# Identity columns of the transposed keys written on the chip, second buffers cleared by ScalarE, first fills and key return due later

## The chip, the core and the metric

The kernel runs on one core of one Trainium2 chip. A core has five engines with instruction queues of their own: TensorE (PE; its weight loads are listed apart as PEld), VectorE (DVE), ScalarE (ACT), GpSimd (POOL) and SyncE (SP), whose queue issues most of the transfers. The transfers run on 16 DMA engines. An engine takes its instructions in the order in which the program names them. The metric is the device time of one execution in microseconds.

## What is computed

Three stages in float32, cut to what matters:

```python
for t in range(S):                      # stage 1: B, H, S, D = 4, 8, 768, 40
    m_new = maximum(f[t] + m, i[t])
    f_stab, i_stab = exp(f[t] + m - m_new), exp(i[t] - m_new); m = m_new
    C = f_stab * C + i_stab * outer(v[t], k[t])      # D x D for each of the 32 heads
    n = f_stab * n + i_stab * k[t]
    y[t] = sigmoid(o[t]) * (C @ q[t]) / maximum(abs(n . q[t]), 1)
x = y as 3072 tokens x 320
logits = x @ w_gate                     # stage 2: 8 experts, 384 tokens each
# all (token, expert) pairs in the order of falling logits: a token takes the first
# expert that still has room
x = relu(x[of expert e] @ w1[e]) @ w2[e]             # 320 -> 1024 -> 320
h = x @ w_in                            # stage 3: 320 -> 2048 -> 320
out = (maximum(h, 0) + alpha * minimum(h, 0)) @ w_out
```

## The kernel before

Stage 1 is `attention()`. The sequence is cut into 9 chunks of L = 86 steps (NCH = 9). A unit is one chunk of one batch entry; 36 units run in order, four to a chunk, and `score(u)`, `value(u - 2)`, `turn(u - 4)` and the rest of the loop's body are issued for each. Within a chunk the recurrence is a masked product, and the state C that enters a chunk is carried as 40 extra rows beside the 86 steps. So the transposed keys KT of a chunk have X = 126 columns for each of 16 pairs of heads: 86 keys, then a 40 x 40 identity that picks the state. A matmul of KT and Q gives pS, VectorE multiplies it by the weights W (ScalarE's exponential of pE, itself a product of cE and aE), and a matmul with V gives pY.

Buffers: Q and KT have R = 2, V has 3, aE and cE have 3. Pairs of heads share one matmul, so Q has zeros where the other head's rows stand, and partitions 80 and up of KT are zero. A load writes 80 partitions of KT; memsets before the first loads clear the rest: for buffer 0 by GpSimd and VectorE (lines 334 to 338), for buffer 1 by GpSimd (lines 385 and 386). In the kernel before, the host lays out `h_kt` with the 40 identity columns in it, and `load_qk(c)` (line 359) loads 80 rows of 16 x 126 numbers, 8064 contiguous bytes each.

The gates are prepared by `gates()`, a generator with a `yield` after each step, in three pieces: chunk 0 (`g0`), chunks 1 to 3 (`g1`) and the rest (`g2`). A piece is a chain on VectorE (two scans, differences, a maximum) and then three times a copy to bf16 on ScalarE (line 298) and a subtraction of it (line 302). The loop over `g0` (from line 387) inserts `fill_a(0)` and `fill_c(0)`, VectorE's copies of the constant rows into aE[0] and cE[0] (lines 373 and 377). Then come `load_a(0)`, three small transfers of `ap` into three rows of aE[0] issued by SP (line 316), `gates_rows(0)` (matmuls, then ScalarE's copy into cE[0], line 312), `prep(0)` (VectorE's copy of the identity `vid` into KR[0], line 347), two more `fill_c`, SP's loads for the next chunk, `fill_a(1)` and the first G0 = 7 steps of `g1`, all before unit 0. SP issues in this order too: q, k and v of chunk 0, the aE rows, kr, og, v, q and k of chunk 1. Later chunks' loads are issued from the units' loop; from unit 8 on, the loop also loads and converts halves of stage 3's weights (`r`, `convert()`).

Stages 2 and 3 are `rest()`. The assignment runs in rounds (`rounds()`), one for each expert: `bisect()` searches the threshold over the table `key`, `pick()`, `compact()` and `gather()` fetch the expert's tokens (xg), `kill()` and `choose()` prepare the next round. `choose()` writes the new keys to DRAM and reads them back in another layout (lines 699 and 700). Beside it TensorE runs the expert's MLP and then the final MLP for its tokens, f from 0 to NF - 1 = 15, with `turn_x()` transposing the next expert's tokens at the last three f. The order of both is written by a planner: `tp` and `td` are its reckoning of TensorE's and VectorE's time, `mm()` adds a matmul to `tp`, and `due()` says whether the next step of the round is issued now. After `choose()` a round yields `keys_at - tp`, so that the next step is issued when `tp` has reached `keys_at`. `rest()` sets `need`, the due time, to `tp` before the first expert, whatever was yielded. If the next expert's gather has not been issued at f = NF - 4, the round is stepped out there, and after it five more microseconds of planned VectorE work.

Of the kernel before, what the change touches and what calls it, by code (L numbers as in the profile page):

```python
# [9 lines left out]
F32 = mybir.dt.float32  # L10
# [78 lines left out]
def host_layout(inp):  # L89
# [8 lines left out]
    def dmajor(a):  # L98
        a = chunks(a).reshape(B, 4, 2, NCH, L, D).transpose(3, 2, 5, 0, 1, 4)
        return np.ascontiguousarray(a).reshape(NCH, 2, D, 16, L)  # L100
# [2 lines left out]
        return np.ascontiguousarray(chunks(a).transpose(2, 3, 0, 1, 4))  # L103

    o["h_q"] = dmajor(q)
    kt = np.zeros((NCH, 2, D, 16, X), np.float32)
    kt[..., :L] = dmajor(k)
    kt[..., L:] = np.eye(D, dtype=np.float32)[:, None, :]
    o["h_kt"] = kt.reshape(NCH, 2 * D, 16, X)
    o["h_kr"] = rows(k).reshape(NCH, L, 32, D)  # L110
    ve = np.ones((NCH, L, 32, D + 1), np.float32)
    ve[..., :D] = rows(v).reshape(NCH, L, 32, D)
# [50 lines left out]
class Kern:  # L163
# [154 lines left out]
    def attention(self):  # L318
        nc, a, tc = self.nc, self.a, self.tc
        with ExitStack() as ctx:  # L320
# [14 lines left out]
            nc.vector.memset(Q[0][:, 1], 0.0)  # L335
            self.gates_fill()
            nc.gpsimd.memset(KT[0][64:], 0.0)
            nc.gpsimd.memset(V[0][64:], 0.0)
            ident = self.identf
            vid = p.tile([128, D], F32, name="vid")  # L340
            nc.vector.tensor_scalar(vid, jp, 0.0, None, op0=OP.is_equal)
            pm = p.tile([128, H * (D + 1)], I32, name="pm")
            wg = p.tile([128, 3, 32], F32, name="wg")
            OG = {}
# [10 lines left out]
            def load_qk(c):  # L355
                r = c % R
                for s in range(2):
                    nc.sync.dma_start(Q[r][D * s:D * s + D, s], a["h_q"][c, s])
                nc.sync.dma_start(KT[r][:2 * D], a["h_kt"][c])

            def load_v(c):
                rows(V[c % RV], a["h_v"][c])
# [9 lines left out]
            def fill_a(r):  # L372
                nc.vector.tensor_copy(self.aE[r].rearrange("p b h l -> p b (h l)"),
                                      self.ae0[:, None, :].to_broadcast([KE, B, H * L]))
# [7 lines left out]
            g0 = self.gates(0, 1, nc.vector)  # L382
            g1 = self.gates(1, 4, nc.vector)
            g2 = self.gates(4, NCH, nc.gpsimd)
            nc.gpsimd.memset(Q[1], 0.0)
            nc.gpsimd.memset(KT[1][64:], 0.0)
            for i, _ in enumerate(g0):
                if i == 4:
                    fill_a(0)
                    fill_c(0)  # L390
            self.load_a(0, nc.sync)
            self.gates_rows(0, ps)
            prep(0)
            fill_c(1)
            fill_c(2)
# [281 lines left out]
    def choose(self, keys, at=320):  # L677

        nc, p, v = self.nc, self.bp, self.v
        B3 = [128, E, 24]  # L680
        self.mine = p.tile([128, 24], F32, name="mine")
        ch = self.rb[:, at:at + 192].rearrange("p (e j) -> p e j", e=E)
        v.tensor_reduce(self.best, self.Lm.rearrange("p e j -> p j e"), axis=AX.X, op=OP.max)
        yield DVE
        v.tensor_tensor(ch, self.Lm, self.best[:, None, :].to_broadcast(B3), op=OP.is_equal)
        yield DVE
        v.tensor_tensor(ch, ch, self.ew[:, :, None].to_broadcast(B3), op=OP.mult)
        yield DVE
        v.tensor_reduce(self.mine, ch.rearrange("p e j -> p j e"), axis=AX.X, op=OP.max)
        if not keys:  # L690
            return
        yield DVE
        v.tensor_tensor(ch, ch, self.mine[:, None, :].to_broadcast(B3), op=OP.is_equal)
        yield DVE
        v.tensor_scalar(ch, ch, 0.5, 2 * OUT, op0=OP.subtract, op1=OP.mult)
        yield DVE
        kt = p.tile(B3, F32, name="ky")
        v.tensor_tensor(kt, ch, self.Lm, op=OP.min)
        nc.sync.dma_start(self.kd.rearrange("e (p j) -> p e j", j=24), kt)
        nc.sync.dma_start(self.key, self.kd.rearrange("e (g t) -> (e g) t", t=192))  # L700
        self.keys += 1
        self.keys_at = self.tp + 5.6

    def count(self, src, thr, op, col=0):
        self.td -= 0.07
# [620 lines left out]
```

## Time and profile before

| | us |
|---|---|
| three runs | 817.33, 814.41, 822.41 |
| median | 817.33 |
| the profiled execution | 814.77 |
| its span, first to last instruction | 812.8 |
| mean granted TensorE clock | 0.959 of full speed |

The profile is of one execution. Attention ends near 177 us, the first round of the assignment fills the time to about 230 us, and the MLPs with the other rounds beside them the rest. A page of the profile sums each engine's busy time; a timeline lists instructions; the chain of waits is followed back from the last instruction of a stretch to what released each; a table by stretch adds the granted clock and what the DMA engines did. DMA shares are of all 16 engines. A packet is one piece that one DMA engine moves.

### The profile page before, as it was taken

To read this page: it belongs to the slowest core of one execution; us is meant where nothing else is said; L and a number is where in the kernel's file an instruction comes from. 1 tells how busy PE (TensorE), PEld (TensorE's weight loads), DVE (VectorE), ACT (ScalarE), POOL (GpSimd) and SP (SyncE) were. 2 spreads that over 40 slices of the span, in tenths; PEclk is the share of its full clock that TensorE was granted. 3 is DMA by queue.
4 is the path that set the end of the run, shared out by engine and by line. 5 is a ranking of instruction groups with operands and counts; after the bars stand their busy time and mean duration, and the time that the engine had idled before them with its cause. 6 is when DMAs were issued, how large, how long until landed. Compare 5 with 4: busy or idle time off the path is not lost.

```text
span 812.8 us, 14924 instructions
## 1 busy us (share of the span) xinstructions
PE 726.5 (89%) x4868; PEld 688.1 (85%) x4868; DVE 566.5 (70%) x2209; ACT 430.2 (53%) x945; POOL 425.9 (52%) x509
## 2 busy tenths in 40 slices
PE   3999998850199999999999999999999999999996
PEld 2998988840088988998999899999989999999996
DVE  8886786889788879877876887787788832322321
ACT  3575565658343564466267436625842764654453
POOL 5565554659572466157239516732950785634133
PEclk9999998975599999999999999999999999999999
DMA  7888988643050041032005003201400333100000
GB/s 177 201 233 218 229 217 222 188 122 108 1 193 2 1 154 65 0 113 83 25 29 167 25 2 112 83 26 42 154 25 1 127 127 100 42 1 25 1 1 25
DMA packets 36730, 74.57 MB, mean 92 GB/s; under 512 B 14576, under 2 KB 18672, under 8 KB 36652
## 3 DMA queue, kind: packets, MB, share of 16 engines
q1 hardware_dynamic: 33532, 64.74, 28.6%
q0 software_dynamic: 2688, 8.65, 3.3%
q8 instruction: 38, 0.62, 0.3%
q14 instruction: 40, 0.33, 0.1%
q10 hardware_dynamic: 432, 0.22, 0.1%
HBM read 64.04 MB, written 9.34 MB: 90 GB/s over the span
## 4 chain that ended last, share of the span: by engine, by line
PE 53%; DVE 15%; POOL 11%; issue 9%; DMA 7%; ACT 3%; SPq 0%; POOLq 0%; DVEq 0%; ACTq 0%
PE ph L1024 22%; PE acc L1024 10%; PE fo L1024 9%; PE pY L461 5%; POOL gl L1161 4%; DVE scr L158 4%; DVE rb L158 3%; PE pS L445 3%; POOL wt L1000 3%; DMA r<-in_h_wf_dram 2%; DMA aE<-ap 2%; POOL w_dt_float32r L957 1%; DVE g L158 1%; DMA k<-in_h_kt_dram 1%; POOL w_dt_float L928 1%
## 5 line engine op out<-in xcount | busy, mean ns | idle before, releaser
L1161 POOL TENSOR_TENSOR gl<-g,gh 128x384 fp32r<-128x384 f32 x127 | 128.0, 1014 | 225.1 <-ACT gh L1160 217.1
L1000 POOL TENSOR_TENSOR wt<-raw,wt 128x384 fp32r<-128x384 f32 (+1 forms) x128 | 118.2, 941 | 32.4 <-ACT wt L999 32.2
L1024 PE MATMUL ph<-yh,wfh 128*128 128x384 f32 x384 | 133.1, 347 | 0.0
L1024 PE MATMUL ph<-yh,w_dt_float32r 128*128 128x384 f32 x360 | 122.1, 339 | 0.0
L1024 PE MATMUL fo<-wfh,gh 128*128 128x320 f32 x384 | 116.4, 313 | 0.4 <-ACT gh L1160 0.4
L158 DVE SCALAR_TENSOR_TENSOR g<-ph,m 128x384 f32<-128x384 f32 x128 | 70.3, 555 | 65.3 <-ACT m L1154 57.7
L1160 ACT ACTIVATE gh<-g 128x384 fp32r<-128x384 f32 x127 | 66.0, 523 | 88.5 <-DVE g L158 88.4
L1024 PE MATMUL fo<-w_dt_float32r,gh 128*128 128x320 f32 x360 | 109.3, 312 | 0.0
L1024 PE MATMUL ph<-xh,wt 128*128 128x384 f32 x384 | 99.5, 343 | 0.6 <-ACT xh L1055 0.6
L1086 ACT ACTIVATE hh<-ph 128x384 fp32r<-128x384 f32 x64 | 31.5, 493 | 115.2 <-PE ph L1024 94.0
L1024 PE MATMUL acc<-hh,wt 128*128 128x384 f32 x320 | 89.1, 343 | 0.0
L1024 PE MATMUL ph<-yl,wfh 128*128 128x384 f32 x256 | 84.1, 339 | 0.0
L1024 PE MATMUL fo<-wfh,gl 128*128 128x320 f32 x384 | 80.1, 312 | 0.5 <-POOL gl L1161 0.5
L1154 ACT ACTIVATE m<-m,al 128x384 f32<-128x384 f32 x119 | 73.4, 617 | 3.9
L1153 ACT ACTIVATE m<-ph 128x384 f32<-128x384 f32 x119 | 57.4, 483 | 32.7 <-PE ph L1024 31.5
L1024 PEld LDWEIGHTS fo<-wfh,gh 128*128 128x128 f32 x384 | 72.2, 188 | 3.0 <-ACT m L1154 1.5
L1024 PEld LDWEIGHTS ph<-yh,wfh 128*128 128x128 f32 x384 | 72.4, 188 | 0.6 <-issue 0.2
L1024 PEld LDWEIGHTS ph<-xh,wt 128*128 128x128 f32 x384 | 69.0, 188 | 1.8 <-issue 1.0
L999 ACT ACTIVATE wt<-raw 128x384 fp32r<-128x384 f32 x128 | 62.8, 514 | 12.6 <-DMA raw<-in_h_we_dram 12.5
L1024 PEld LDWEIGHTS fo<-w_dt_float32r,gh 128*128 128x128 f32 x360 | 67.9, 188 | 1.1 <-issue 1.0
L1024 PEld LDWEIGHTS ph<-yh,w_dt_float32r 128*128 128x128 f32 x360 | 67.9, 188 | 0.7 <-issue 0.7
L461 PEld LDWEIGHTS pY<-v,dk 126*126 126x126 f32 (+1 forms) x576 | 67.2, 191 | 0.7
(237 smaller groups left out, 1636.1 us busy)
## 6 DMA issues: line engine op xcount, KB each, us to landing
raw<-in_h_we_dram SPq DMA_DIRECT2D x64, 384.0 KB
r<-in_h_wf_dram SPq DMA_DIRECT2D x32, 352.0 KB
k<-in_h_kt_dram SPq DMA_DIRECT2D x9, 630.0 KB
xd<-x SPq DMA_DIRECT2D x36, 120.0 KB
q<-in_h_q_dram SPq DMA_DIRECT2D x18, 215.0 KB
v<-in_h_v_dram SPq DMA_DIRECT2D x9, 410.0 KB
og<-in_h_o_dram SPq DMA_DIRECT2D x9, 400.0 KB
kr<-in_h_kr_dram SPq DMA_DIRECT2D x8, 400.0 KB
```

The source lines that it names most:

```text
L158: return f(out, *args, **kw)
L445: nc.tensor.matmul(pS[:, 2 * j:2 * j + 2, :], KT[r][:, 4 * b + 2 * s + j, :], Q[r][:, :, 4 * b + 2 * s + j, :], start=True, stop=True)
L461: nc.tensor.matmul(pY[:M, h, :], dk[:, h, :M], V[c % RV][:, 8 * b + h, :], start=True, stop=True)
L928: nc.gpsimd.tensor_tensor(w, w, sg, op=OP.mult)
L999: nc.scalar.activation(w[:, :384], r, AF.Copy)
L1000: nc.gpsimd.tensor_tensor(w[:, 384:], r[:, :n], w[:, :n].bitcast(F32), op=OP.subtract)
L1024: self.nc.tensor.matmul(out, w, x, **kw)
L1086: nc.scalar.activation(hh, ph, AF.Relu)
L1153: nc.scalar.activation(m, ph, AF.Relu, scale=-1.0)
L1154: nc.scalar.activation(m, m, AF.Copy, scale=alpha)
L1160: nc.scalar.activation(gh, g, AF.Copy)
L1161: nc.gpsimd.tensor_tensor(gl, g, gh.bitcast(F32), op=OP.subtract)
```

## The change

The host no longer puts the identity into `h_kt`; its rows hold 16 x 86 numbers, and the load writes 16 pieces of 86 numbers to each of 80 partitions, beside the columns 86 to 125 that it leaves alone. The chip writes the identity: VectorE adds two blocks of the 128 x 128 identity into `idk`, GpSimd copies it into KT[0] after that buffer's memset, ScalarE into KT[1]. The clears of Q[1] and of KT[1]'s partitions 64 to 127 go from GpSimd to ScalarE (a copy scaled by zero), the first ahead of the gates of chunk 0, the second behind `gates_rows(0)`. `vid` is computed by GpSimd instead of VectorE. In the loop over `g0` the two fills move back: `fill_a(0)` from step 4 to 5 and `fill_c(0)` from step 4 to 7. In `choose()` the due time of the next round becomes the later of `tp` and `td` plus 6.6 instead of `tp` plus 5.6.

```diff
--- before.py
+++ after.py
@@ -103,10 +103,7 @@
         return np.ascontiguousarray(chunks(a).transpose(2, 3, 0, 1, 4))
 
     o["h_q"] = dmajor(q)
-    kt = np.zeros((NCH, 2, D, 16, X), np.float32)
-    kt[..., :L] = dmajor(k)
-    kt[..., L:] = np.eye(D, dtype=np.float32)[:, None, :]
-    o["h_kt"] = kt.reshape(NCH, 2 * D, 16, X)
+    o["h_kt"] = dmajor(k).reshape(NCH, 2 * D, 16, L)
     o["h_kr"] = rows(k).reshape(NCH, L, 32, D)
     ve = np.ones((NCH, L, 32, D + 1), np.float32)
     ve[..., :D] = rows(v).reshape(NCH, L, 32, D)
@@ -335,10 +332,13 @@
             nc.vector.memset(Q[0][:, 1], 0.0)
             self.gates_fill()
             nc.gpsimd.memset(KT[0][64:], 0.0)
+            ident = self.identf
+            idk = p.tile([2 * D, D], F32, name="idk")
+            nc.vector.tensor_tensor(idk, ident[:2 * D, :D], ident[:2 * D, D:2 * D], op=OP.add)
+            nc.gpsimd.tensor_copy(KT[0][:2 * D, :, L:], idk[:, None, :].to_broadcast([2 * D, 16, D]))
             nc.gpsimd.memset(V[0][64:], 0.0)
-            ident = self.identf
             vid = p.tile([128, D], F32, name="vid")
-            nc.vector.tensor_scalar(vid, jp, 0.0, None, op0=OP.is_equal)
+            nc.gpsimd.tensor_scalar(vid, jp, 0.0, None, op0=OP.is_equal)
             pm = p.tile([128, H * (D + 1)], I32, name="pm")
             wg = p.tile([128, 3, 32], F32, name="wg")
             OG = {}
@@ -356,7 +356,7 @@
                 r = c % R
                 for s in range(2):
                     nc.sync.dma_start(Q[r][D * s:D * s + D, s], a["h_q"][c, s])
-                nc.sync.dma_start(KT[r][:2 * D], a["h_kt"][c])
+                nc.sync.dma_start(KT[r][:2 * D, :, :L], a["h_kt"][c])
 
             def load_v(c):
                 rows(V[c % RV], a["h_v"][c])
@@ -382,14 +382,17 @@
             g0 = self.gates(0, 1, nc.vector)
             g1 = self.gates(1, 4, nc.vector)
             g2 = self.gates(4, NCH, nc.gpsimd)
-            nc.gpsimd.memset(Q[1], 0.0)
-            nc.gpsimd.memset(KT[1][64:], 0.0)
+            zero = ident[:, 1:2]
+            nc.scalar.activation(Q[1].rearrange("p s g l -> p (s g l)"), zero.to_broadcast([128, 32 * L]), AF.Copy, scale=0.0)
             for i, _ in enumerate(g0):
-                if i == 4:
+                if i == 5:
                     fill_a(0)
+                if i == 7:
                     fill_c(0)
             self.load_a(0, nc.sync)
             self.gates_rows(0, ps)
+            nc.scalar.activation(KT[1][64:].rearrange("p g x -> p (g x)"), zero[64:].to_broadcast([64, 16 * X]), AF.Copy, scale=0.0)
+            nc.scalar.activation(KT[1][:2 * D, :, L:], idk[:, None, :].to_broadcast([2 * D, 16, D]), AF.Copy)
             prep(0)
             fill_c(1)
             fill_c(2)
@@ -699,7 +702,7 @@
         nc.sync.dma_start(self.kd.rearrange("e (p j) -> p e j", j=24), kt)
         nc.sync.dma_start(self.key, self.kd.rearrange("e (g t) -> (e g) t", t=192))
         self.keys += 1
-        self.keys_at = self.tp + 5.6
+        self.keys_at = max(self.tp, self.td) + 6.6
 
     def count(self, src, thr, op, col=0):
         self.td -= 0.07
```

## Rows read from the trace of the kernel before

**Rows 1.** page: busy time, share, instructions; DMA busy in tenths of 40 slices

```profile
PE 726.5 (89%) x4868; PEld 688.1 (85%) x4868; DVE 566.5 (70%) x2209; ACT 430.2 (53%) x945; POOL 425.9 (52%) x509
...
DMA  7888988643050041032005003201400333100000
```

**Rows 2.** TensorE's waits, 44 to 140 us: total us, times, longest us

```profile
PE pE L438 <- DMA aE<-ap: 2.4, 2, 1.8
PE pS L445 <- ACT KL L517: 2.2, 1, 2.2
```

**Rows 3.** chain of waits: start us, length us, what

```profile
68.47 7.79 DMA aE<-ap
```

**Rows 4.** by stretch: busy us (instructions) each engine, clock, DMA share, GB/s

```profile
76.00:80.00 4.00, 3.61 (x16) 3.60 (x16) 1.31 (x4) 2.42 (x6) 2.67 (x4) 0.59 0.72 185
...
132.00:136.00 4.00, 4.00 (x40) 3.68 (x40) 2.25 (x8) 0.79 (x2) 2.10 (x4) 0.50 1.04 269
```

**Rows 5.** timeline, VectorE: start us, length us, line, operation, count

```profile
6.05 2.84 DVE L373 COPY aE<-ae 113x2752 bf16<-113x2752 bf16 x1
8.81 1.94 DVE L377 COPY cE<-ce 113x504 bf16<-113x504 bf16 x1
...
11.00 0.24 DVE L302 TENSOR_TENSOR cum<-cum,ap 32x86 f32<-32x86 f32 x1
...
11.97 0.81 DVE L347 COPY kr<-vid 126x1280 f32<-126x1280 f32 x1
12.71 0.47 DVE L377 COPY cE<-ce 113x504 bf16<-113x504 bf16 x2
13.11 0.86 DVE L373 COPY aE<-ae 113x2752 bf16<-113x2752 bf16 x1
...
16.22 0.68 DVE L293 TENSOR_TENSOR_SCAN cum<-keep,fg 32x258 f32<-32x258 f32 x1
```

**Rows 6.** timeline, same stretch: GpSimd, then ScalarE; idle before in brackets

```profile
4.48 1.22 POOL L338 MEMSET v<- 62x1312 f32 x1
5.76 2.40 POOL L385 MEMSET q<- 128x2752 f32 x1
...
6.15 0.27 ACT L298 ACTIVATE ap<-cum 32x86 bf16<-32x86 f32 x1 [2.22 <-DVE cum L293]
...
13.31 0.45 ACT L312 ACTIVATE cE<-pc 24x344 bf16<-24x344 f32 x1 [0.96 <-PE pc L310]
...
17.71 0.43 ACT L440 ACTIVATE W<-pE 126x344 f32<-126x344 f32 x1
```

**Rows 7.** lines by form, 0 to 180 us: busy us, mean ns, idle before

```profile
L957 POOL TENSOR_TENSOR w-1_dt_float32r<-w_dt_float,wfh 128x704 fp32r<-128x704 f32 x1 | 1.7, 1677 | 0.0
...
L956 ACT ACTIVATE wfh<-w_dt_float 128x704 fp32r<-128x704 f32 x2 | 1.6, 784 | 3.3 <-PE pk L525 3.3
...
L476 POOL COPY x<-x 86x64 f32<-86x64 f32 x35 | 10.3, 294 | 2.2
```

**Rows 8.** DMA queue of 7-10, 496-498, 230.9-231.9 us: packets, MB, share

```profile
q1 hardware_dynamic: 117, 0.65, 98.6%
...
q1 hardware_dynamic: 273, 0.74, 98.7%
...
q1 hardware_dynamic: 1040, 0.10, 71.5%
```

**Rows 9.** DMA issues, 44 to 131 us: count, KB each

```profile
k<-in_h_kt_dram SPq DMA_DIRECT2D x5, 630.0 KB
```

**Rows 10.** source line 700: who waited for it, us, times

```profile
  DVE rb L158: 3.1, 3
```

**Rows 11.** timeline: GpSimd's gather issue, then TensorE's transposes of it

```profile
358.51 0.99 POOL L973 DMA_INDIRECT xg<-xd,ids  x1
...
366.69 0.49 PE L1052 MATMUL ptr<-identf,xg 128*128 128x128 f32 x3
...
369.72 0.49 PE L1052 MATMUL ptr<-identf,xg 128*128 128x128 f32 x3
```

## What the change does to the time, told before it was run

> **What bounds the kernel now.** I read the page first. TensorE is busy for 89% of the span, and the packets keep the DMA engines seven to nine tenths busy in the first slices, where attention runs, and little after [rows 1]. So one question falls to each part: what delays TensorE in attention, and whether the long stage behind it, the two MLPs, can move at all.
>
> The waits of TensorE between 44 and 140 us come next [rows 2]. They are few; the two longest are 2.4 us for the small loads into aE and 2.2 us for ScalarE. Attention's middle is a stretch in which TensorE nearly keeps pace with the DMA queue. The chain of waits shows what is behind the first: aE, a load of three rows of `ap`, is 7.79 us under way [rows 3], because it stands in the queue behind the large loads. The table by stretch adds the price that the list of waits hides: the granted clock is 0.59 from 76 to 80 us and 0.50 from 132 to 136 [rows 4]; the first is a mixture of the two levels 2.4 and 1.2 GHz, the second is the lower one throughout. TensorE had idled shortly before both. Counted as four microseconds times what is missing to 1, the two stretches lose 1.64 and 2.00, together 3.6 us.
>
> The timeline of the start shows another limit. Until the first weights W are made at 17.71 us ScalarE waits for VectorE's gate values, and VectorE spends 2.84 us on the copy fill_a(0) and 1.94 us on fill_c(0) between cum and the rest of the gate chain; the same copies later take 0.86 us and 0.47 us for two [rows 5]. GpSimd clears the second buffers just then, Q[1] from 5.76 us on [rows 6].
>
> **The start, part by part.** Taken off GpSimd: the memsets of Q[1], 2.40 us [rows 6], and of KT[1]. Added there: the identity copy into KT[0], 80 x 640 elements, not in the trace. GpSimd's copy of 64 elements takes 294 ns and its product of 704 elements 1677 ns [rows 7]; 640 elements lie near the second, so I take 1.5 us (bounds 0.3 and 1.7). It stands before V[0]'s memset and delays that by as much, so v(0) is issued some 1.5 us later on SP, and what is queued behind it, load_a(0), waits for the gates anyway. Also moved to GpSimd is vid, read by prep alone. VectorE gets idk, one 80 x 40 addition, 0.24 us by the 32 x 86 operations of the chain [rows 5]; it lies where vid lay.
>
> VectorE's chain from the end of cum, which lets ScalarE go at 6.15 us [rows 6], to prep(0) at 11.97 us [rows 5] is 5.8 us now. Afterwards: ig 0.24, fill_a(0), two subtractions 0.48 (0.24 each), fill_c(0) 0.24 (half of 0.47), two subtractions 0.48. The identity copy pushes GpSimd's V[0] memset to end near 7.2 us, so fill_a(0) meets part of it: between 0.86 and 2.84 I take 1.5, nearer to the free one because only its first microsecond has a rival. Sum 2.94, with 0.2 for ScalarE's copies in between 3.15; prep(0) begins 2.7 us earlier. Bounds: with 2.84 for fill_a and idk waiting out half of GpSimd's 1.5 us copy besides, 0.6; with 0.86 for fill_a, 3.3.
>
> The slowing itself is what [rows 5] and [rows 6] show: 2.84 against 0.86 us for one instruction. The Trainium skill, page "SBUF — State Buffer", section "Who interferes with whom", says that a VectorE copy in a two-port mode and GpSimd block each other and that ScalarE never waits; this trace agrees with the first half (2.84 against 0.86), and no run here yet shows the second. By that rule the clears cost nothing on ScalarE but their own time, as the next sum has it too.
>
> ScalarE takes three new instructions. Its rows give 273 ns for 86 elements and 784 for 704 [rows 6, 7], hence 0.83 ns an element: 2752 elements 2.5 us, 2016 elements 1.9 us, 640 elements 0.7 us. Q[1]'s clear starts when ScalarE's table load ends, at 3.93 us (6.15 less the idle 2.22) [rows 6], and ends near 6.4, 0.25 after cum; fill_a(0) covers that. KT[1]'s two stand behind cE(0), which ends 2.7 us earlier, at 11.1: they last until 13.7. Behind them wait gates' copies for chunks 1 to 3, whose cum ends at 16.90 now [rows 5] and at 14.2 then. Cover 0.5 us; were the two twice as long, W would lose 2.1 us of the gain. load_qk(1) waits on SP for these clears; its data are used four units later. So the first W comes 2.7 us earlier, and what follows is bound by TensorE until DMA binds.
>
> **The key loads.** Nine loads of 80 rows x 8064 B become nine of 80 x 16 pieces of 344 B: 630 KB become 430, 80 packets become 1280. No such packet is in the trace, so I bound it from three stretches that hold nearly one kind each [rows 8]. Mean of a packet is 16 engines x length x share / packets. The 80-row loads (7 to 10 us): 47.3 engine-us for 0.65 MB, 13.7 B/ns. The 128-row loads (496 to 498): 31.6 for 0.74 MB, 23.4 B/ns; 129 ns for 3072 B once the small ones (273 less 0.74 MB / 3072 B) are set apart at 11 ns. 96 B packets: 11.0 ns. A line through the last two is 7.2 ns + 0.040 ns/B, 20.9 ns for 344 B. One row of a partition costs now 8064/13.7 = 589 ns. Later: if only bytes count, 5504/13.7 = 402; if the crowding of 80-row loads (1.74, the ratio of 23.8 to 13.7) stretches all of a packet, 16 x 36.4 = 582; if it stretches the bytes alone, 16 x (7.2 + 23.8) = 496. Each engine carries five rows, so a load gets shorter by 0.93, 0.03 or 0.47 us. I take 0.5.
>
> The Trainium skill, page "DMA: Bandwidth & Descriptors", section "Specifications", speaks against this edit: transfers need at least 512 B for line rate, and below it the engine reads, modifies and writes. Its sense here is a rival below. The trace does not bear it out for its smallest pieces: 96 B cost 11.0 ns [rows 8].
>
> Five of the loads are issued between 44 and 131 us [rows 9]: 5 x 0.5 = 2.5 us off the queue's lateness, out of 4.6 us of waits in [rows 2]. Of the 3.6 us of lost clock I take back 1.5: the shorter of the idle times may stop being one, the other need not. Together 4.0 us, bounds 0.2 and 8.2. What is late next is VectorE, which carries attention's end.
>
> **The keys' return.** In the rounds the next search is emitted when tp reaches keys_at. The last step leaves td about 0.4 us ahead of tp, so the new line delays it by 1.4 us (1.0 and 0.4). Three of the returns kept VectorE waiting, 3.1 us in all [rows 10]; the first is outside, because rest() overwrites the due time. In the MLPs VectorE has slack before most matmuls, so I take 0.5 us (bounds -1 and +1.5).
>
> **Sum.** The profiled execution took 814.77 us, span 812.8. 814.8 - 2.7 - 4.0 - 0.5 = 807.6 us. The median of the three runs is 817.33, 2.6 higher; on it the sum is 810.1. A median is what will stand against a median, so I say 809.5.
>
> **Rivals.** *Key loads hidden or no shorter:* the lower bound of 0.03 us. For it speaks that TensorE idles little; against it the two aE waits. 814.8 - 2.7 - 0.5 - 0.2 = 811.4 on the profile's time, 814 on the median.
>
> *The stalls vanish whole:* both waits (4.6) and all the lost clock (3.6) go. For it speaks that all stand behind the queue; against it that 2.5 us do not cover 4.6. 814.8 - 2.7 - 8.2 - 0.5 = 803.4, or 806.
>
> *Small packets dear, slower than before:* place, the queue from 44 to 131 us. If a piece of 344 B pays its bytes twice in the crowd, it costs 7.2 + 2 x 23.8 = 54.8 ns, a row 877 ns, a load 1.44 us more, five loads 7.2: 814.8 + 7.2 - 3.2 = 818.8, or 821.4. It decides from 45 ns a piece on: there 25 rows' excess (16 x 45 - 589) eats the 3.2 us. The 96 B row speaks against it, and that none of those went into the crowded rows speaks for it. It is also how the Trainium skill's 512 B rule named above would act.
>
> *Later keys reach the gather:* a gather not yet emitted three feed-forward blocks before the expert's end makes TensorE wait while the round is stepped out, then 5 us more. The third expert's first gather starts at 358.51 us, its transposes at 366.69, and one block is 3.03 us [rows 11]; the test comes near 363.6, slack 5.1 us against a delay of 1.4. It decides above 5.1 us and would give 807.6 + 5 = 812.6 or more; the delays of later rounds add up, 1.4 us each, which is why it keeps a chance.
>
> **How the numbers follow.** Forecast 0.54 (its own range 805 to 814), key loads without gain 0.22, stalls gone 0.14, dear packets 0.06, late gather 0.04. A measurement of this kernel tells about 1% from no change, 8.2 us. Faster by over that: all of stalls gone and the better part of the forecast's, 0.14 + 0.24 = 0.38. Slower by over 1% needs packets of some 65 ns (16 x 65 - 589 = 451 ns, 11.3 us over 25 rows, less 3.2) or both of the last two: 0.04. The rest, 0.58. The range 803 to 816 leaves out the dear packets and the tails.
>
> **What would show it.** Right: first W at about 15 us; fill_a(0) under 2 us; key packets of 344 B at 25 to 37 ns; the aE wait near 76 us under 1 us; no VectorE wait for a key return after the first. Wrong at the start: W still near 17 us, with ScalarE in KT[1]'s clears while gates' cum is done. Wrong in the middle: packets of 45 ns, longer waits for aE, more stretches at 0.5 clock. Wrong at the end: a wait of TensorE before the transposes of a gather.

## The result, and the profile after

| | before | after |
|---|---|---|
| median of 4 runs each, same chip (lowest to highest) | 819.87 us (814.41 to 825.80) | 808.62 us (807.25 to 809.98) |
| ratio of the times, 95% interval | | 0.9891 (0.9849 to 0.9932) |
| profiled execution: time, span, mean clock | 814.77, 812.8, 0.959 | 807.28, 805.5, 0.961 |
| first W of chunk 0 starts | 17.71 us | 14.04 us |
| first W of chunk 3 | 59.4 us | 56.9 us |
| first W of chunk 8 | 148.5 us | 138.4 us |
| first matmul of the first expert | 232.25 us | 222.60 us |
| from there to the end of the span | 580.6 us | 582.9 us |

The change makes the kernel 1.1% faster, 0.7 to 1.5% by the interval. Run again beside 29 runs of the kernel before, it gave a ratio of 0.9898 (0.9856 to 0.994). Ratios and means below leave out the few runs that were over 1.5% above the fastest of their kernel. The forecast was 809.5 us, and on the profiled execution 807.6; measured were 808.62 and 807.28. But the table says that the parts of the sum do not agree as well as the sum. In the profiled executions 3.7 us come from the start (forecast 2.7), 6.0 us more until the first expert (forecast 4.0), and 2.3 us are given back in the MLPs (forecast: 0.5 gained). -3.7 - 6.0 + 2.3 = -7.4, against 814.77 - 807.28 = 7.5.

The page of the changed kernel, the same rows as [rows 1]:

```profile
PE 722.2 (90%) x4868; PEld 684.9 (85%) x4868; DVE 562.3 (70%) x2209; ACT 434.6 (54%) x948; POOL 422.8 (52%) x509
...
DMA  8989889551320140042014004202400343100000
```

ScalarE is busy 4.4 us longer with three instructions more; the DMA engines are up to a tenth busier in most of the first slices. TensorE's busy time falls by 4.3 us with the same 4868 instructions. Most of it is the clock: between 44 and 140 us the lower level held for 10.2 us before and not at all after, and in the MLPs after for 3.4 us.

The timeline of the start (start us, length us, engine, line, operation, idle before in brackets), to be laid beside [rows 5] and [rows 6]:

```profile
3.95 2.50 ACT L386 ACTIVATE q<-identf 128x2752 f32<-128x2752 f32 x1
4.60 0.78 POOL L338 COPY k<-idk 80x640 f32<-80x640 f32 x1
5.44 1.19 POOL L339 MEMSET v<- 62x1312 f32 x1
5.47 0.33 DVE L290 TENSOR_TENSOR_SCAN cum<-keep,fg 32x86 f32<-32x86 f32 x1
5.99 1.37 DVE L373 COPY aE<-ae 113x2752 bf16<-113x2752 bf16 x1
...
7.61 0.45 DVE L377 COPY cE<-ce 113x504 bf16<-113x504 bf16 x1
...
8.30 0.81 DVE L347 COPY kr<-vid 126x1280 f32<-126x1280 f32 x1
...
10.12 1.88 ACT L394 ACTIVATE k<-identf 64x2016 f32<-64x2016 f32 x1
12.03 0.74 ACT L395 ACTIVATE k<-idk 80x640 f32<-80x640 f32 x1
13.26 0.42 ACT L295 ACTIVATE ap<-cum 32x258 bf16<-32x258 f32 x1 [0.50 <-DVE cum L290]
...
14.04 0.77 ACT L443 ACTIVATE W<-pE 126x344 f32<-126x344 f32 x2
```

fill_a(0) takes 1.37 us where it took 2.84, fill_c(0) 0.45 where it took 1.94, and prep(0) (the copy into kr) starts 3.67 us earlier. The last clear of KT[1] ends at 12.77 us, and ScalarE then waits 0.50 us for cum: the clears are covered, with half a microsecond to spare.

TensorE's waits from 44 to 140 us (total us, times, longest us), and then the two stretches of [rows 4] with a third one (stretch: length, busy us of PE, PEld, DVE, ACT, POOL with instructions, clock, DMA share, GB/s):

```profile
PE pS L448 <- DVE LT L567: 1.0, 3, 0.5
PE pS L448 <- ACT KL L520: 0.9, 1, 0.9
```

```profile
76.00:80.00 4.00, 3.86 (x33) 3.57 (x32) 2.69 (x8) 1.94 (x6) 2.16 (x4) 1.00 1.07 271
132.00:136.00 4.00, 4.00 (x37) 3.99 (x36) 1.72 (x4) 1.74 (x6) 1.51 (x2) 1.00 0.70 207
370.00:374.00 4.00, 3.55 (x13) 3.24 (x13) 2.11 (x15) 0.21 (x1) 3.22 (x5) 0.57 0.00 0
```

In this execution the wait for aE is gone from the list, that for KL fell from 2.2 to 0.9 us [rows 2], and both stretches run at the full clock, 1.00 for 0.59 and 0.50 [rows 4]. The third row is new: in the MLPs, at 370 us, the clock is 0.57. The timeline there names what came before it:

```profile
368.25 0.56 DVE L155 SCALAR_TENSOR_TENSOR g<-ph,m 128x384 f32<-128x384 f32 x1 [1.69 <-POOL gl L1164]
...
370.45 0.17 PE L721 MATMUL rb<-acc,c_blk 128*128 128x3 bf16 x1 [2.06 <-DVE rb L155]
```

TensorE waits 2.06 us for a step of the top-k search on VectorE, and that step stands behind the instruction for `g`, which had waited 1.69 us for GpSimd. That is where the later return of the keys put it. The wait for the keys themselves (line 703, line 700 before) fell from 3.1 us in three waits [rows 10] to 0.4 in one, as meant.

### The profile page after: what moved, and what is told of

The parts are those of the page before. It is cut to its first block, busy times and chain, and to the rows that moved or that the text cites. A ratio compares the mean times of both kernels' runs of the same rounds, so it can differ in the third digit from the quotient of the medians.

```text
span 805.5 us, 14932 instructions
## 1 busy us (share of the span) xinstructions
PE 722.2 (90%) x4868; PEld 684.9 (85%) x4868; DVE 562.3 (70%) x2209; ACT 434.6 (54%) x948; POOL 422.8 (52%) x509
## 4 chain that ended last, share of the span: by engine, by line
PE 49%; DVE 14%; POOL 9%; issue 8%; ACT 5%; DMA 2%; SPq 0%; POOLq 0%; DVEq 0%; ACTq 0%
PE ph L1027 23%; PE acc L1027 11%; PE fo L1027 10%; POOL gl L1164 4%; DVE scr L155 3%; DVE rb L155 2%; PE pY L464 2%; POOL wt L1003 2%; DVE g L155 2%; POOL w_dt_float32r L960 1%; ACT m L1157 1%; PE pS L448 1%; ACT gh L1163 1%; POOL w_dt_float L931 1%; ACT m L1156 1%
## 5 line engine op out<-in xcount | busy, mean ns | idle before, releaser
L1027 PE MATMUL acc<-hl,wt 128*128 128x384 f32 x192 | 66.6, 347 | 1.0 <-DVE hl L155 1.0
```

Source lines behind the costliest of these rows:

```text
L1027: self.nc.tensor.matmul(out, w, x, **kw)
```

## The experiments

The theory to be tested had three parts: the start gains by the clears' leaving GpSimd; the key loads are shorter because they carry fewer bytes, though in more packets; the later keys cost time where they were meant to gain. The rivals: the small packets gain nothing, or cost; all of the gain is the start's; the later keys gain. The runs came in three groups (the first four below; the next three and tp + 4.6; the last four), each beside 29 runs of the kernel before, median 817.07, 815.25 and 815.65 us. Ratios are to these. Every kernel computes the whole result.

### The old due time in the changed kernel

```diff
-        self.keys_at = max(self.tp, self.td) + 6.6
+        self.keys_at = self.tp + 5.6
```

> The changed kernel with the due time of the keys' return as before (tp + 5.6). By the prediction's sum the later due time saved 0.5 us, so this kernel should be 0.5 us slower than the changed one, at some 0.5 us above its 807.3 us. By the reading of the changed kernel's trace the later due time cost 2 to 2.5 us (a wait of TensorE of 2.06 us at 370 us that the kernel before does not have, and a stretch at the lower clock behind it, against 1.8 us of VectorE's waits gone), so it should be 2 us or more faster than the changed one, with no wait over 1 us in the MLPs. The waits of VectorE for the returned keys come back by both.

Measured: 807.93 us, ratio 0.9883 (0.983 to 0.9937); profiled 805.13. The MLPs take 580.8 us where they took 582.9, and TensorE's 2.06 us wait at the third return is not there. The gain of the change does not come from the third edit; whether that edit costs anything in the time lies within the interval. The expectation of no wait over 1 us in the MLPs was missed: there is one of 1.48 us at the second return of the keys. The kernel before has it too, and the changed kernel has not (in its profile the same step waits 0.21 us):

```profile
305.69 0.16 PE L718 MATMUL rb<-acc,c_blk 128*128 128x3 bf16 x1 [1.42 <-DVE rb L158]
```

### The new due time alone

```diff
-        self.keys_at = self.tp + 5.6
+        self.keys_at = max(self.tp, self.td) + 6.6
```

> The kernel before with the later due time of the keys alone. By the prediction's sum 0.5 us faster than before; by the reading of the changed kernel's trace 2 to 2.5 us slower, with attention unchanged (the last search table's transposes at 176.2 us) and a new wait of TensorE of about 2 us near the start of the third expert. A third theory: what the due time does in the MLPs hangs on where the round happens to stand, and then the difference here need not have the sign that the reverse edit has in the changed kernel.

Measured: 817.74 us, ratio 1.0014 (0.9979 to 1.005). The time does not tell it from nothing. In its profiled execution the MLPs take 581.6 us for 580.6, the wait at the second return is gone, and the timeline has the new wait at the same place of the third:

```profile
380.57 0.16 PE L718 MATMUL rb<-acc,c_blk 128*128 128x3 bf16 x1 [2.05 <-DVE rb L158]
```

So the new wait belongs to this edit and to no other, and the edit takes another wait away.

### The key loads alone

The loads of 344 B pieces in the kernel before; the identity columns of both buffers are written by GpSimd behind its memsets, the clears stay where they were.

```diff
+            idk = p.tile([2 * D, D], F32, name="idk")
+            nc.vector.tensor_tensor(idk, ident[:2 * D, :D], ident[:2 * D, D:2 * D], op=OP.add)
+            nc.gpsimd.tensor_copy(KT[0][:2 * D, :, L:], idk[:, None, :].to_broadcast([2 * D, 16, D]))
...
-                nc.sync.dma_start(KT[r][:2 * D], a["h_kt"][c])
+                nc.sync.dma_start(KT[r][:2 * D, :, :L], a["h_kt"][c])
...
+            nc.gpsimd.tensor_copy(KT[1][:2 * D, :, L:], idk[:, None, :].to_broadcast([2 * D, 16, D]))
```

> The kernel before with the key loads of 344 B pieces alone; GpSimd writes the identity columns of both buffers, its clears and the fills stay where they were. By the prediction's sum attention ends 4.0 us earlier, less what GpSimd's two added copies hold up at the start (0 to 1.5 us). If the loads alone account for what the changed kernel gained between the first W and attention's end, 6.4 us. If the gain came from the earlier start, which lets the loads be issued sooner, 0 to 1 us, and the waits for aE near 76 us and the stretches at the lower clock stay.

Measured: 811.44 us, ratio 0.9921 (0.9891 to 0.995), although the first W comes 1.1 us later (18.82), since GpSimd's two copies (0.71 and 0.81 us) delay VectorE's gate steps and fills. In the profiled execution the first expert starts at 228.12 us, 4.1 earlier, which is 5.2 behind the start, between the 4.0 of the sum and the 6.4 of the other reading. The rival that the key loads are hidden, or bring no gain, falls here. TensorE's waits, 44 to 140 us:

```profile
PE pS L446 <- ACT KL L518: 0.8, 1, 0.8
PE pE L439 <- DMA aE<-ap: 0.7, 1, 0.7
```

The wait for aE is 0.7 for 2.4 and that for KL 0.8 for 2.2 [rows 2].

### The start alone

The changed kernel with the wide loads of before and the old due time; no idk.

```diff
-            nc.gpsimd.tensor_copy(KT[0][:2 * D, :, L:], idk[:, None, :].to_broadcast([2 * D, 16, D]))
...
-                nc.sync.dma_start(KT[r][:2 * D, :, :L], a["h_kt"][c])
+                nc.sync.dma_start(KT[r][:2 * D], a["h_kt"][c])
...
-        self.keys_at = max(self.tp, self.td) + 6.6
+        self.keys_at = self.tp + 5.6
```

> The changed kernel with the key loads and the due time as before: 8064 B pieces with the host's identity, ScalarE's clears, the fills moved back, vid on GpSimd. By the prediction's sum the first W at 15.0 us and attention's end 2.7 us earlier than before; by the changed kernel's trace 3.7 us (first W at 14.0). If the earlier start also removed the waits behind the DMA queue, 6 to 10 us; if the queue takes the start's gain back because wide loads bind again, under 2 us.

Measured: 813.11 us, ratio 0.9929 (0.9899 to 0.9959). In its profiled execution the first W starts at 14.10 us, 3.6 earlier, but the first expert at 230.2, only 2.1 earlier. The waits of TensorE, 44 to 140 us, in this execution:

```profile
PE pE L440 <- DMA aE<-ap: 3.6, 3, 2.3
PE pS L447 <- ACT KL L519: 2.2, 1, 2.2
```

TensorE gets ahead of the queue and waits 3.6 us for aE, where it waited 2.4 [rows 2]. But the times do not show that the queue takes part of the start back: 0.71% of 817 is 5.8 us (3.3 to 8.3), no less than the 3.6 of the start.

### The start's two edits apart

```diff
-                if i == 4:
+                if i == 5:
                     fill_a(0)
+                if i == 7:
                     fill_c(0)
```

> The kernel before with the two first fills moved back (steps 5 and 7) alone; GpSimd clears the second buffers as before. If GpSimd's memsets beside them are what makes the fills slow, fill_a(0) still takes 2.5 us or more, fill_c(0) too is held up, and the first W comes at most 0.6 us earlier than 17.7. If the place in the order is what counts, the first W comes 2 us or more earlier.

Measured: 815.07 us, ratio 1.0001 (0.9966 to 1.0036). The first W starts at 16.71 us, 1.0 earlier: more than the 0.6 that the reading by GpSimd's memsets allowed, and half of the 2 that the other asked for.

```diff
-            nc.gpsimd.memset(Q[1], 0.0)
-            nc.gpsimd.memset(KT[1][64:], 0.0)
+            zero = ident[:, 1:2]
+            nc.scalar.activation(Q[1].rearrange("p s g l -> p (s g l)"), zero.to_broadcast([128, 32 * L]), AF.Copy, scale=0.0)
...
             self.gates_rows(0, ps)
+            nc.scalar.activation(KT[1][64:].rearrange("p g x -> p (g x)"), zero[64:].to_broadcast([64, 16 * X]), AF.Copy, scale=0.0)
```

> The kernel before with the clears of Q[1] and KT[1] on ScalarE alone; fills, vid, key loads and due time as before. If GpSimd's memsets are what makes the fills slow, fill_a(0) takes 0.9 to 1.4 us, fill_c(0) under 0.5, and the first W comes 3 us or more earlier, near 14.5. If the place of the fills is what counts, W gains under 1.5 us. The end of the attention stage follows by at most 2 us, as it did where the start alone was changed.

Measured: 812.51 us, ratio 0.9957 (0.9927 to 0.9987). The fills in the timeline, with the fills moved alone and then with the clears moved alone:

```profile
6.32 2.56 DVE L373 COPY aE<-ae 113x2752 bf16<-113x2752 bf16 x1
...
9.12 1.63 DVE L377 COPY cE<-ce 113x504 bf16<-113x504 bf16 x1
```

```profile
3.95 2.50 ACT L386 ACTIVATE q<-identf 128x2752 f32<-128x2752 f32 x1
...
6.05 0.85 DVE L373 COPY aE<-ae 113x2752 bf16<-113x2752 bf16 x1
6.82 0.27 DVE L377 COPY cE<-ce 113x504 bf16<-113x504 bf16 x1
```

Moved a step or two, the fills still meet GpSimd's memsets and take 2.56 and 1.63 us. With the clears on ScalarE they take 0.85 and 0.27 us; ScalarE's clear of 2.50 us lies beside the first 0.4 us of them. For the length of the fills it is the engine of the clears that matters, and of the two edits tested alone only this one shows in the time. The first W starts at 15.22 us, 2.5 earlier, a little short of the 3 expected, and at 14.10 with both edits (and with vid moved). In the profiled execution with the clears alone, 2.1 us above its median, the first expert starts at 232.43 us, no earlier than before; the gain of 0.4% stands in the runs' times only.

### Small packets at equal bytes

The kernel before, its host rows padded by 8 B a piece, so that the same 8064 B a row go as 16 pieces of 504 B.

```diff
-    kt = np.zeros((NCH, 2, D, 16, X), np.float32)
+    kt = np.zeros((NCH, 2, D, 16, 128), np.float32)
...
-                nc.sync.dma_start(KT[r][:2 * D], a["h_kt"][c])
+                nc.sync.dma_start(KT[r][:2 * D], a["h_kt"][c][:, :, :X])
```

> The kernel before with the same bytes of keys and identity, but loaded as 80 x 16 pieces of 504 B (the host's rows have a gap of 8 B after each piece) instead of 80 of 8064 B. By the prediction's line for pieces with crowding on the bytes alone a load gets 0.42 us longer (16 x 42 = 672 against 589 ns for a row), attention ends 2 us later over five loads. With crowding on all of a piece 0.84 us and 4 us. If the packets' own time overlaps between neighbours on one engine, so that only bytes count, no change within 1 us. If pieces under 512 B pay their bytes twice, a row is 16 x 77 = 1230 ns, a load 3.2 us longer, attention ends 10 us or more later.

Measured: 819.79 us, ratio 1.0051 (1.0024 to 1.0077), some 4 us slower. Cutting the rows costs time, and the change has to earn this back by the bytes that it leaves out. The total is what the expectation had with crowding on all of a piece (0.84 us a load, 4 us over five loads), and twice the bytes (3.2 us a load, 16 over five) is far off. But the loads have not become longer, as that sum has it: from its first to its last packet a load of 504 B pieces takes 6.3 us in the mean of nine, and a load of 8064 B rows 6.3 to 6.8 in the five profiles that have them. So the total is met by another way than the one it was reckoned from. The issue of a key load keeps SP busy for 0.60 us, where it took 0.32. SP's waits for key loads, 44 to 140 us, before and with the pieces:

```profile
SPq L906 <- DMA k<-in_h_kt_dram: 10.9, 5, 2.7
```

```profile
SPq L906 <- DMA k<-in_h_kt_dram: 14.4, 5, 3.1
```

With the narrow pieces alone this wait is 9.2 us, in the changed kernel 9.5. It does not account for the 4 us: in the four other profiles with wide loads it is 6.1 to 10.2, and all of SP's waits in the stretch add up to 44.2 us before and 43.9 with the pieces. The stretch 44 to 140 us in five kernels follows (before, this one, the key loads alone, the start alone, after; columns as above):

```profile
44.00:140.00 96.00, 89.48 (x840) 84.23 (x839) 70.10 (x194) 57.63 (x148) 53.43 (x81) 0.95 0.88 220
```

```profile
44.00:140.00 96.00, 89.53 (x826) 84.68 (x826) 68.92 (x192) 57.16 (x147) 52.47 (x81) 0.92 0.93 218
```

```profile
44.00:140.00 96.00, 92.09 (x896) 86.76 (x895) 72.79 (x201) 59.53 (x153) 56.07 (x85) 0.98 0.91 216
```

```profile
44.00:140.00 96.00, 88.49 (x813) 83.19 (x810) 69.10 (x193) 56.39 (x144) 51.40 (x79) 0.95 0.88 222
```

```profile
44.00:140.00 96.00, 92.58 (x916) 87.37 (x908) 75.57 (x211) 62.21 (x160) 56.97 (x88) 1.00 0.91 215
```

The instructions that TensorE gets through in the same 96 us rise and fall with the clock: 826 at 0.92, 840 and 813 at 0.95, 896 at 0.98, 916 at 1.00. Times 96 us, what is missing to 1 is 7.7, 4.8, 1.9, 4.8 and 0 us. These are single executions, that of the pieces (824.20 us) the second slowest of twelve, and they do not tell whether TensorE did less because of the clock or lost the clock because it had less to do.

The times of all runs, each with its own mean clock, allow an estimate. Call a run's lost clock its time multiplied by what is missing to full clock. Among the runs of the kernel before, the time grows by some 0.6 us for each us of lost clock. In the mean the pieces lose 40.3 us where the runs beside them lose 36.2, and the key loads alone 32.1 for 37.8. So some 2 of the 4 us that the pieces cost, and some 3.5 of the 6 that the key loads gain alone, go with the clock. Where the rest of the pieces' cost arises stays open.

### The due time: earlier still, and the changed kernel again

```diff
-        self.keys_at = max(self.tp, self.td) + 6.6
+        self.keys_at = self.tp + 4.6
```

> The changed kernel with the due time of the keys' return a microsecond earlier than before (tp + 4.6). If VectorE's waits for the keys are hidden, the MLPs last 580 to 581 us as with tp + 5.6 and VectorE's waits for keys grow to 4 us or more in all. If such a wait is passed on to TensorE, the MLPs get 1 to 3 us longer, with waits of TensorE for VectorE behind each return.

> The changed kernel with tp + 4.6. If the MLPs' length follows the due time, 578 to 579 us as in its first profile, and some 4 us less time than the changed kernel; if that profile was one lucky execution, 580 to 581 us like tp + 5.6 and about 2 us less.

The two others differ by the constant alone, 3.6 and 2.6, and one run is the changed kernel unaltered:

> The changed kernel with tp + 3.6. If the gain of an earlier due time goes on, the MLPs last under 578 us. If VectorE's wait for the keys (about 1 us a return more than at 4.6, 7 us or more in all) is now passed on to TensorE, 580 us or more, with waits of TensorE for VectorE's hl or g behind the returns.

> The changed kernel with tp + 2.6. By the first reading no longer than with 3.6; by the second 2 us or more longer than with 4.6, VectorE's waits for keys 10 us or more in all.

> The changed kernel once more, beside the next three, which differ from it in the due time of the keys' return alone (max(tp, td) + 6.6 here). By the reading that the later due time costs, TensorE has a wait of about 2 us in the MLPs behind the third return, as in its first profile and in the kernel with this edit alone, and the MLPs last 582 to 583 us. If that wait was the accident of one execution, it is absent.

| due time | median us | ratio (interval) | MLPs, us | VectorE's waits for keys, us (times) |
|---|---|---|---|---|
| max(tp, td) + 6.6, first | 808.62 | 0.9891 (0.9849 to 0.9932) | 582.9 | 0.4 (1) |
| the same, again | 807.96 | 0.9898 (0.9856 to 0.994) | 581.2 | 1.1 (1) |
| tp + 5.6 | 807.93 | 0.9883 (0.983 to 0.9937) | 580.8 | 2.0 (3) |
| tp + 4.6, first | 806.51 | 0.9881 (0.9844 to 0.9919) | 578.4 | 3.5 (4) |
| the same, again | 806.78 | 0.99 (0.9864 to 0.9935) | 579.2 | 3.9 (4) |
| tp + 3.6 | 811.99 | 0.996 (0.9929 to 0.9992) | 585.0 | 6.5 (6) |
| tp + 2.6 | 822.08 | 1.0062 (1.0034 to 1.009) | 597.0 | 16.5 (6) |

VectorE's waits for the keys grow the earlier the search is emitted, and the MLPs are shortest where these waits are not yet zero. Rows of the timeline show the two ends, in the changed kernel run again and at tp + 2.6:

```profile
370.40 0.16 PE L721 MATMUL rb<-acc,c_blk 128*128 128x3 bf16 x1 [2.06 <-DVE rb L155]
```

```profile
573.07 0.36 DVE L155 TENSOR_SCALAR rb<-key 128x192 int32<-128x192 int32 x1 [2.91 <-DMA key<-kd]
...
575.14 0.16 PE L721 MATMUL rb<-acc,c_blk 128*128 128x3 bf16 x1 [3.50 <-DVE rb L155]
```

Too late, and TensorE waits for a search step that stands behind the MLP's own work on VectorE; too early, and it waits for a search that waits for the keys. The first wait, 2.05 or 2.06 us at the third return, is in the three profiles with 6.6 and not in those with 5.6 or 4.6. The reverse holds for the wait at the second return: 1.33 to 1.48 us in all nine profiles with 5.6 or 4.6, and in none with 6.6. With tp + 5.6 the MLPs take 580.3 to 581.0 us in seven profiles, the kernel before among them, so that 578.4 and 579.2 lie outside this spread. The version with tp + 4.6 has the shortest spans of all, 801.7 and 801.6 us against 805.5 and 804.1; its ratio is not to be told from that of the changed kernel.

Four expectations were missed. The first run of tp + 4.6 has shorter MLPs (578.4 us) than either reading had it. The second is 1.2 us faster in the median than the changed kernel beside it, not 4. In the changed kernel run again the wait at the third return is there, but the MLPs last 581.2 us, not 582 to 583. And with tp + 3.6 TensorE's waits for `hl` and `g` do not grow: its waits for search steps do, 7.5 us in all (none over 0.9) for 4.8 with tp + 4.6.

## Why the prediction was right, and where its steps were not

**The start: mechanism right, and 0.3 or 1.0 us too small, by the execution.** In the first profile the first W comes 3.67 us earlier, beyond the bound of 3.3. From the end of cum to prep(0) the prediction set 3.15 us, and 2.50 were measured (5.80 to 8.30): fill_a(0) took 1.37 for the 1.5 assumed and fill_c(0) 0.45 for 0.24, which nearly cancel; but the subtractions of 0.24 us start 0.15 to 0.17 after one another (7.28, 7.45, 7.61), where they were counted at full length. A chain of short instructions on one engine costs their spacing, not the sum of their durations. And cum, which the prediction kept where it was, ended 0.31 us earlier (5.80 for 6.11). 0.65 + 0.31 is the missing microsecond.

But the changed kernel's start is in seven profiles (its own two, and the five with another due time). The first W comes at 14.04 to 14.07 us in three and at 14.74 to 14.76 in four, 2.95 us earlier than before and within the bound. In the four, two of VectorE's gate steps meet GpSimd's instructions, as in the changed kernel run again:

```profile
4.60 0.71 POOL L338 COPY k<-idk 80x640 f32<-80x640 f32 x1
4.68 0.73 DVE L286 TENSOR_TENSOR fg<-fg,gm 32x85 f32<-32x85 f32 x1
5.38 1.19 POOL L339 MEMSET v<- 62x1312 f32 x1
5.44 1.17 DVE L288 TENSOR_SCALAR fg<-fg 32x86 f32<-32x86 f32 x1
6.65 0.33 DVE L290 TENSOR_TENSOR_SCAN cum<-keep,fg 32x86 f32<-32x86 f32 x1
```

In the first profile the same two steps start at 4.56 us, just ahead of the copy, and at 4.83, and take 0.23 and 0.60. So the identity copy that went to GpSimd meets the gates' chain ahead of cum, which the prediction reckoned with for idk and fill_a(0) alone, and a tenth of a microsecond at the start of a step decides over 0.7 us. That vid's move brought cum forward is not shown: with vid moved and without the identity copies (the start alone) cum ends at 6.08 us, as before.

GpSimd's identity copy was taken at 1.5 us and took 0.71 to 0.82: its nearest row was a product of two inputs, and a copy is a good deal cheaper. ScalarE's clears took 2.50, 1.88 and 0.74 us for 2.5, 1.9 and 0.7 foretold, and their covers held, the second with 0.50 us left, as said.

The second half of the rule cited from the Trainium skill, page "SBUF — State Buffer", section "Who interferes with whom", that ScalarE never waits for the other two, agrees with these runs: Q[1]'s clear took 2.50 us whether GpSimd ran a memset beside it and VectorE a copy at its end (the clears alone) or GpSimd a copy and a memset (the changed kernel).

**The key loads: right direction, wrong currency.** The step took a packet's mean time for a share of the engine's time, and expected 25 to 37 ns for 344 B. Measured over the nine loads of the changed kernel were 37.8 ns, so that a row of 16 takes 605 ns, no less than the 589 of before. By that step's own rule the loads had not got shorter, and yet the kernel with narrow pieces alone is 0.8% faster, and from first to last packet a load takes 5.1 us in the mean where it took 6.4 (5.6 with the narrow pieces alone). The mean times of a packet came out near the step's line with crowding on all of it, 37.8 ns for 36.4 with 344 B and 49.7 for 47.6 with 504 B; adding them up was wrong. What the step lacked is in the queue's view (packets, MB, share of 16 engines): 7 to 8.5 us in the changed kernel, and 6.1 to 10 us in the kernel with pieces of 504 B:

```profile
q1 hardware_dynamic: 822, 0.35, 137.5%
```

```profile
q1 hardware_dynamic: 1338, 0.85, 103.2%
```

A share above 100% means that packets of one engine overlap in time. The durations of single packets can then not be added to an engine's time, and the formula of [rows 8], which gave 98.6% for the wide rows, does not carry over. A first sign of it is in [rows 4], 1.04 from 132 to 136 us, with a load of wide rows issued there. That the bytes left out do the gaining is shown by two kernels: with 16 pieces and 8064 B a row the time rises by 0.5%, with 16 pieces and 5504 B it falls by 0.8%.

On the rule cited from the Trainium skill, page "DMA: Bandwidth & Descriptors", section "Specifications" (at least 512 B for line rate): the pieces of 504 B lie below it and did cost, 0.51% (0.24 to 0.77). No run here has pieces just above 512 B, so whether it is that limit or the number of packets that costs is not told apart. A price of twice the bytes, 7.2 us more over five loads by the prediction's sum, is excluded for 344 B by the gain.

**The lost clock: counted too small before, and got back whole in one profile of seven.** The prediction counted 3.6 us from two stretches of four microseconds. By the trace the lower level held for 3.4 us from 76.7 and for 6.8 from 131.3, 10.2 us at 0.50, which is 5.1 us lost. From chunk 3 to chunk 8 the first Ws lie 89.2 us apart before and 81.6 after. Less the waits for aE and KL, and less half of the time at the lower level, this stretch comes out at 78.0 to 81.7 us in eleven profiles, where as measured it runs from 81.6 to 98.1:

| kernel | chunk 3 to 8, us | waits for aE and KL | half of the time at 0.50 | rest | first expert starts |
|---|---|---|---|---|---|
| before | 89.2 | 4.6 | 5.1 | 79.4 | 232.25 |
| pieces of 504 B | 98.1 | 4.8 | 15.4 | 78.0 | 241.63 |
| start alone | 90.2 | 5.8 | 5.1 | 79.3 | 230.16 |
| key loads alone | 84.8 | 1.5 | 1.7 | 81.6 | 228.12 |
| after | 81.6 | 0.9 | 0 | 80.7 | 222.60 |
| changed, again | 84.4 | 2.0 | 3.4 | 79.0 | 222.91 |
| changed, tp + 5.6 | 83.4 | 2.9 | 1.7 | 78.8 | 222.57 |
| changed, tp + 4.6 | 84.7 | 2.4 | 3.4 | 78.9 | 223.32 |
| the same, again | 84.0 | 1.9 | 3.4 | 78.7 | 222.44 |
| changed, tp + 3.6 | 84.8 | 2.5 | 3.4 | 78.9 | 225.04 |
| changed, tp + 2.6 | 82.2 | 1.0 | 0.4 | 80.8 | 222.56 |

So the step of 4.0 us behind the start was 6.0 in the first profile: 7.6 here, of which the stretches beside it take back 1.6 (42.8 us from chunk 0 to chunk 3 for 41.7 before, 84.2 from chunk 8 to the first expert for 83.7). There the rival "the stalls vanish whole" was close to the truth. In the other six the step was 4.2 to 6.7, the KL wait 1.0 to 2.4 us, and the lower level lasted 3.4 or 6.8 us ahead of the long stretch at 0.50 in which attention ends. In every profile of the changed kernel that is less than in the five with 8064 B rows (10.2 to 17.1 us). But the start of the first expert does not follow it: 222.60 with none, 222.44 and 225.04 with 6.8. What the clock gives between chunks 3 and 8 is taken back beside it, and how much of the step is the clock's is not shown by these stretches.

**The keys: wrong sign.** -0.5 was foretold with a bound of +1.5; +2.3 was measured in the first profile, +0.6 in the second (581.2 for 580.6) and +1.0 with this edit alone. The step counted what VectorE waits for and what the gather might lose, and not what TensorE waits for. Delaying a search moves its steps to other places in VectorE's order; one came to stand behind `g`, and a wait of TensorE of 2.06 us followed at the third return, while one of 1.4 at the second went; in the first profile that came with 3.4 us at the lower clock (1.7 us) on top: 0.7 more idle time on balance (10.1 for 9.4 us in the MLPs) and 1.7 make the 2.3, but for 0.1. In the measured times the edit can't be told from nothing (ratio 1.0014, 0.9979 to 1.005).

**The gather.** The rival of a late gather shows in no run: behind the first expert's gather TensorE stands before a gather's transposes for 0.2 us at most, in any profile. The first expert's, which the due time does not reach, has up to 0.6 us.

**The sum.** That it came so near is luck in part: the start and the step behind it were reckoned too small and the keys too well, 3.0 us more gain and 2.8 us more loss in the first profile. The choice of 809.5 from 807.6 and 810.1 went by a median of 817.33; with a fourth run it was 819.87, and the gain in medians was 11.3 us, where 7.8 had been forecast (7.7 in the second comparison, 815.65 to 807.96). By its own bound of 1% the change is faster (1.1%), which had 0.38, and not within 1%, which had 0.58; the interval holds both.

**What stays open.** In the profiled executions the two parts alone bring the first expert forward by 4.1 and 2.1 us and together by 9.65; in the six other profiles of the changed kernel by 7.2 to 9.8, so this recurs. In the medians it is not so: 0.79% and 0.71% alone, 1.17% together with the old due time (0.63 to 1.7), which is the sum or less. The executions that were profiled differ in rank: the fastest of six with the old due time and in the changed kernel run again, but above the median of its runs with the start alone. So the excess may be one of the executions profiled. Nor is it settled how much of the key loads' gain is the shorter queue itself and how much is clock that the shorter queue saves; the estimate above gives the clock some 3.5 of 6 us.

## What to carry to other kernels

Before a transfer is cut into more packets to save bytes, measure the same cut at equal bytes: here it cost 0.5%, and only the 32% fewer bytes of each load made the edit a gain of 0.8%. Clears that run beside a VectorE copy belong on an engine that does not slow it (here ScalarE, 0.85 us for 2.84), and whatever goes to GpSimd in exchange must be checked against the VectorE steps beside it (here 0.7 us of the start, in four of seven profiles). One profile is one execution: a stretch that it explains to the tenth should be looked up in the others before a cause is drawn from it. A due time in a hand-written order has two bad ends, and is set by what the bound engine waits for on either side, not by making one wait zero.

## What the runs showed of the hardware that was not expected

Packets of 344 B on one DMA engine overlap: the share is 137.5% of 16 engines from 7 to 8.5 us, so that their mean duration (37.8 ns) says little of throughput. The issue of a load cut into 1280 pieces kept SP busy for 0.60 us, and that of one in 80 rows for 0.32.

The granted clock does not follow a wait in the same way each time. After the wait of 2.06 us at 370 us it was 0.50 for 3.4 us in one execution of the changed kernel (370.5 to 373.9). After the same wait in another execution, from 370 to 374 us, it stayed at 1.00, as it did after the wait of 2.05 us with the new due time alone:

```profile
370.00:374.00 4.00, 3.60 (x23) 3.37 (x23) 3.35 (x21) 0.82 (x3) 3.21 (x5) 1.00 0.00 0
```

TensorE got through 23 matmuls there, and through 13 in the other. Between executions of one program this alone is worth 1.7 us a time.
